# Final sums opened earlier and gMLP run ahead of the first keys in a cached attention block beside a gMLP mixer

## The chip, the cores and the metric

The kernel runs on 1 core of one Trainium2 chip. The metric is device time in microseconds (us): the median of several executions. A profile of one further execution gives a trace of every engine. The engines are named PE (TensorE, matrix products), PEld (its weight loads), DVE (VectorE), ACT (ScalarE), POOL (GpSimd) and SP (SyncE, which here only issues transfers). Sixteen DMA engines move the data between HBM and the on-chip memory.

## The reference

The output is the sum of the input, a decode step of attention over a cache, and a gMLP mixer, for 4 batch rows of width 640. Keys and values have 32 heads, 4096 positions and 128 columns each, in bf16: 134 MB of keys and as much of values.

```python
def _A_ref(x, k_cache, v_cache, wq, wo):
    B, Sq, D = x.shape
    Hq, Dh = (32, 128)
    ...
    q = (lambda x, *d: x.transpose(*d))((x @ wq).reshape(B, Sq, Hq, Dh), 0, 2, 1, 3)
    ...
    scores = jnp.einsum('bhqd,bhkd->bhqk', q, k) * Dh ** (-0.5)
    p = _softmax(scores, axis=-1)
    o = jnp.einsum('bhqk,bhkd->bhqd', p, v)
    return (lambda x, *d: x.transpose(*d))(o, 0, 2, 1, 3).reshape(B, Sq, Hq * Dh) @ wo

def _B_ref(x, w_in, w_sp, b_sp, w_out):
    ...
    z = _gelu(jnp.einsum('bsd,df->bsf', x, w_in))
    z1 = z[..., :Fh].copy()
    z2 = _layernorm(z[..., Fh:], axis=-1)
    g = jnp.einsum('ts,bsf->btf', w_sp, z2) + b_sp[None, :, None]
    return jnp.einsum('bsf,fd->bsd', z1 * g, w_out)
x = A_x
xn = _layernorm(x, axis=-1)
return x + _A_ref(xn, A_k_cache, A_v_cache, A_wq, A_wo) + _B_ref(xn, B_w_in, B_w_sp, B_b_sp, B_w_out)
```

The query is one position long (Sq = 1), so nearly all the bytes are read once and used once. wq is 640 x 4096, wo 4096 x 640, w_in 640 x 1728, w_out 864 x 640.

## The kernel before

**Tiles.** Heads are taken in 4 groups of 8; a tile is one batch row of one group, so there are 16 tiles (`NT`). The keys of a tile are one run of 8,192 KB (64 KB in each of 128 partitions), its values another. A tile of keys is worked on in 4 quarters.

**The ring.** One large buffer, `ring`, has 11 units of 16 KB per partition (L91). A run of keys takes 4 units, a run of values 4. `place_k` (L102) puts the keys of tile 0, 2, 4... at units 3 to 6 (`K_EVEN`) and those of tile 1, 3, 5... at units 0 to 3; the two share unit 3, and `quarters` (L105) gives the order in which a tile's quarters are worked on, so that the shared unit comes free first. Values lie at units 7 to 10 (`V_HOME`). At the start wq holds units 0 to 2, and gMLP's weights units 9 and 10 (`W_UNIT`); at the end the last values take units 3 to 6 and wo units 0 to 2.

**The queue.** All large transfers go out on SP's queue in the order in which they are written down in `loads` (L189 to L201): k0, gMLP's weights, k1, v0 in two halves, k2, then v1, k3, v2, k4 and so on, the last values in two halves, wo in four pieces. wq goes out ahead of them all (L110). `pump` (L206) issues the next entries of the list as far as the units that they need have been given up in the program's order; the issue itself then waits on SP until the engines have really finished with these units. SP works in order: what stands behind a waiting issue waits too. k0 goes out in two halves (`load_k`, L148), gMLP's weights in four transfers (`load_w`, L132: w_in 2,160 KB, w_out 960 KB, and two edge pieces of 60 KB).

**One quarter of keys.** `product` (L537, DVE) multiplies the quarter in place with the query, `fold` (L546, DVE) adds the upper half of the 128 columns to the lower, `sums` (L552, PE) adds 64 columns down to 8 with 8 products by the identity into one of two `s_ps` buffers, and `row_sums` (L567, DVE) adds the 8. After the fourth quarter `lane_max` (L577: DVE's `m`, a small ACT step, a PE product into `max_ps`) and `exps` (L585: DVE's `nb`, then the exponential on ACT) make the probabilities `p`; `deal` (L602, ACT) spreads them over the heads' columns, or `deal_part` (L615, DVE) in the last tile.

**Values.** `blocks` (L626, PE) multiplies the dealt probabilities of tile i - 1 with its values, in two halves, behind the second and third quarter of tile i; `gather` (L642) brings the result together. Per group of four tiles `group_den`, `group_rden`, `group_norm`, `group_turn` and `group_pick` divide by the sum of the exponentials and turn the result; `group_den` (L690) has a POOL step `own_sum` and a PE product `den`.

**gMLP.** `gmlp_in` (ACT copies of edge columns, 90 PE products with w_in), `gmlp_gelu`, `gmlp_stats` and `gmlp_out` (18 PE products with w_out, added to `out_ps`) are written into tile 0: behind its third quarter's sums, behind its fourth's, and between `lane_max(0)` and `exps(0)`.

**The end.** `open_finals` (L668) takes both `s_ps` buffers for the final sums, clears them on DVE (L673), copies the sums so far (the input and gMLP) from `out_ps` to `rest` (L676, DVE) and puts them into the final sums with PE products (L680). It comes after the last tile's deals. Then follow `group_den`, `group_rden`, the last `blocks`, `gather`, the group's steps, and `pair_proj` (L748), 128 PE products with wo's two halves. Two copies and two stores end the program.

The engines work in the order in which the program is written (`manual_schedule`, L760), each in its own.

Of the kernel before, what the change touches and what calls it, by code (L numbers as in the profile page):

```python
# [9 lines left out]
FP32 = mybir.dt.float32  # L10
# [10 lines left out]
def kernel(  # L21
# [14 lines left out]
    nc = tc.nc  # L36
    P = nc.NUM_PARTITIONS
    Bsz, Sq, D = A_x.shape
# [10 lines left out]
    HG = H // HT  # L49
    NT = HG * Bsz  # L50
# [3 lines left out]
    NQ = 4  # L54
# [3 lines left out]
    UNIT = QC * Dh  # L58
    UV = UC // QC
# [12 lines left out]
    NOH = D // 2  # L72
# [9 lines left out]
    work = ctx.enter_context(tc.tile_pool(name="work", bufs=1))  # L82
# [16 lines left out]
    K_EVEN, V_HOME = NQ - 1, 2 * NQ - 1  # L99
    W_UNIT, WO_UNIT = V_HOME + UV, 0  # L100

    def place_k(i):  # L102
        return 0 if i % 2 else K_EVEN

    def quarters(i):  # L105
        return tuple(reversed(range(NQ))) if place_k(i) == 0 else tuple(range(NQ))

    wq_flat = ring[:, 0 : DC * HD]
    wq_sb = wq_flat.rearrange("p (c n) -> p c n", n=HD)
# [38 lines left out]
    def load_k(i):  # L148
        t = units(place_k(i), NQ)
        step = (UV if i == 0 else NQ) * UNIT  # L150
        for e in range(0, NQ * UNIT, step):
            nc.sync.dma_start(out=t[:, e : e + step], in_=run_view(A_k_cache, i)[:, e : e + step])
        k_tiles[i] = t.rearrange("p (c d) -> p c d", d=Dh)

# [24 lines left out]
    def plan(keys, first, fn, *args):  # L179
        loads.append((keys, first, fn, args))  # L180

    def plan_k(i):
        plan([("k", i, q) for q in range(NQ)], place_k(i), load_k, i)

    def plan_v(i, part, unit, n=1):
        keys = [("v", i, part + e // UV) for e in range(n * UV)]
        plan(keys, unit, load_v, i, part, unit, n)

    plan_k(0)  # L189
    plan(["w"] * UV, W_UNIT, load_w)  # L190
    plan_k(1)
    plan_v(0, 0, V_HOME)
    plan_v(0, 1, V_HOME + UV)
    plan_k(2)
    for i in range(1, NT - 1):
        plan_v(i, 0, V_HOME, 2)
        if i + 2 < NT:
            plan_k(i + 2)
# [5 lines left out]
    used = set()  # L204

    def pump():  # L206
        while loads:
            keys, first, fn, args = loads[0]
            spots = range(first, first + len(keys))
            for u, key in zip(spots, keys):  # L210
                if u in holder and holder[u] != key and holder[u] not in used:
                    return
            holder.update(zip(spots, keys))
            fn(*args)
            loads.pop(0)
# [140 lines left out]
    def out_sum(half):  # L356
        return out_ps[OG * half : OG * half + Bsz, :]
# [26 lines left out]
    def gmlp_in():  # L384
        zT = gm["zT"] = ps_pv.tile([P, 2, NFC, Bsz], FP32, tag="pv", name="zT")
        w_cols = w_sb[:, 0 : DC * F].rearrange("p (a f) -> p a f", a=DC * 2)
        nc.gpsimd.memset(w_edge[:], 0.0)
        for g in range(2):
            at = NFF * P + g * TL * TR
            cols = w_cols[:, :, at : at + TL * TR].rearrange("p a (k e r) -> p a r e k", e=NW, r=TR)  # L390
            for r in range(TR):
                nc.scalar.copy(
                    out=w_edge[:, :, r, g * CW : g * CW + TL].rearrange(
                        "p a (e k) -> p a e k", e=NW
                    ),
                    in_=cols[:, :, r],
                )
        for t in range(2):
            w_t = w_cols[:, :, 0 : NFF * P].rearrange("p a (f k) -> p a k f", k=NFF)
            for k in range(NFC):  # L400
                for c in range(DC):
                    nc.tensor.matmul(  # L402
                        out=zT[: P if k < NFF else TN, t, k, :],
                        lhsT=w_t[:, 2 * c + t, k, :] if k < NFF else w_edge[:, 2 * c + t, k - NFF, :],
                        rhs=xnT[:, c, 0:Bsz],
                        start=(c == 0),
                        stop=(c == DC - 1),
                    )
# [104 lines left out]
    def stage_q(hg):  # L513
        ps = slice(hg % 2 * 2 * QW, (hg % 2 + 1) * 2 * QW)
        qr_ps = ps_m.tile([HT * Bsz, Dh], FP32, tag="m", name="qr_ps")
        for hh in range(QH):
            nc.tensor.matmul(  # L517
                out=qr_ps[:],
                lhsT=place[ps, hh, :],
                rhs=q_sb[ps, hg // 2, hh * Dh : (hh + 1) * Dh],  # L520
                start=(hh == 0),
                stop=(hh == QH - 1),
            )
        q_rows = small.tile([HT * Bsz, Dh], BF16, name="q_rows")
        nc.scalar.copy(out=q_rows[:], in_=qr_ps[:])  # L525
        qb_ps = ps_m.tile([P, Bsz, Dh], FP32, tag="m", name="qbc_ps")
        for b in range(Bsz):
            nc.tensor.matmul(
                out=qb_ps[:, b, :], lhsT=q_lanes[:, b, :], rhs=q_rows[:], start=True, stop=True
            )  # L530
        qbcs[hg] = small.tile([P, Bsz, Dh], BF16, name="qbc")
        nc.scalar.copy(out=qbcs[hg][:], in_=qb_ps[:])
# [130 lines left out]
    def out_last(part):  # L663
        half, c = divmod(part, 2)
        at = OG * (2 * c + half)
        return finals[c][at : at + Bsz, 0:NOQ]

    def open_finals():  # L668
        rest = work.tile([P, NOH], FP32, tag="early", name="rest")
        for c in range(2):  # L670
            f = ps_s.tile([P, QC, RW], FP32, name="s_ps")
            finals.append(f[:].rearrange("p c d -> p (c d)"))
            nc.vector.memset(finals[c][column_half(c), 0:NOQ], 0.0)  # L673
        for half in range(2):
            ps = slice(OG * half, OG * half + Bsz)
            nc.vector.tensor_copy(out=rest[ps], in_=out_sum(half))  # L676
        for part in range(CG):
            half, c = divmod(part, 2)
            ps = slice(OG * half, OG * half + Bsz)
            nc.tensor.matmul(  # L680
                out=out_last(part),
                lhsT=ident_f[ps, ps],
                rhs=rest[ps, c * NOQ : (c + 1) * NOQ],
                start=True,
                stop=False,
            )
# [73 lines left out]
    with tc.manual_schedule(engines={E.PE, E.DVE, E.Activation, E.SP}):  # L760
        pump()
        stage_q(0)
        LAST = NT - 1
        for i in range(NT):
            order = quarters(i)
            ends = i // Bsz - 1 if i > Bsz and i % Bsz == 1 else None
            for n, q in enumerate(order):
                product(i, q)
                fold(i, q)
                if n:  # L770
                    row_sums(i, order[n - 1])
                if ends is not None and n == 1:
                    group_rden(ends)
                    group_norm(ends)
                elif ends is not None and n == 2:
                    group_pick(ends)
                sums(i, q)
                if i == 0 and n == 2:
                    gmlp_in()
                elif i == 0 and n == 3:  # L780
                    gmlp_gelu()
                if i % Bsz == Bsz - 1 and n == 1 and i // Bsz + 1 < HG:
                    stage_q(i // Bsz + 1)
                if ends is not None and n < 2:
                    (group_den, group_turn)[n](ends)
                if i and n in (1, 2):
                    blocks(i - 1, n - 1)
                    if n == 2:
                        gather(i - 1)
            row_sums(i, order[-1])  # L790
            lane_max(i)
            if i == 0:
                gmlp_stats()
                gmlp_out()
                used.add("w")
                pump()
            exps(i)
            if i == LAST:
                deal_part(i, 0)
                deal_part(i, 1)  # L800
            else:
                deal(i)
        assert not loads
        open_finals()
        group_den(HG - 1)
        group_rden(HG - 1)
        blocks(LAST, 0)
        blocks(LAST, 1)
        gather(LAST)
        group_norm(HG - 1)  # L810
        group_turn(HG - 1)
        group_pick(HG - 1)
        for j in range(NP):
            pair_proj(j)

        res = work.tile([P, NOH], BF16, name="res")
        nc.scalar.copy(out=res[:OUT, 0:NOQ], in_=finals[0][column_half(0), 0:NOQ])
        nc.vector.tensor_copy(out=res[:OUT, NOQ:NOH], in_=finals[1][column_half(1), 0:NOQ])
        out_v = out.flatten_outer_dims()
        nc.scalar.dma_start(out=out_v[:, NOH:D], in_=res[OG : OG + Bsz])  # L820
        nc.sync.dma_start(out=out_v[:, 0:NOH], in_=res[0:Bsz])
# [30 lines left out]
```

## Time and profile before

| what | value |
|---|---|
| median of 3 runs | 661.39 us (661.39 to 661.72) |
| the profiled execution | 662.4 us |
| its span, first to last instruction | 660.3 us |
| busy: DVE | 496.9 us (75%) |
| busy: PE | 317.4 us (48%) |
| busy: ACT | 86.1 us (13%) |
| busy: POOL | 8.5 us (1%) |
| mean granted PE clock | 0.672 |
| bytes read from HBM | 282.24 MB, 427 GB/s over the span |

Times in the views of the profile count from the span's start. A busy share is an average over the whole span; it does not say which engine a stretch waits for. In a timeline line, "x8" means that so many instructions were merged, the arrow shows what is written from what, and the bracket at the end gives the idle time of that engine before the line and what ended it. SP's lines are the issues of transfers; the data lands later.

### The profile page before, as it was taken

Reading aid. Unit: us, or ns where it says so; the run is one execution under the profiler, and the core shown is the slowest. Engines: PE = TensorE matmul, PEld = TensorE weight load, DVE = VectorE, ACT = ScalarE, POOL = GpSimd, SP = SyncE. Lnnn points to the kernel's source line nnn. Section 1 sums busy time; section 2 is a strip of 40 time slices with the busy share of each in tenths; the row PEclk is TensorE's granted clock in tenths of the full one; section 3 lists DMA queues with packets and bytes.
Section 4 is the critical chain, followed back from the end, with each engine's and each line's share of the span. In section 5 each row is a group of like instructions: output and inputs, shape, how many; then the busy total and the mean of one; then the engine's idle time right before and its main releaser. Section 6 shows DMA issues by size and latency. Waiting matters only on the chain.

```text
span 660.3 us, 4884 instructions
## 1 busy us (share of the span) xinstructions
PE 317.4 (48%) x2095; PEld 146.0 (22%) x2095; DVE 496.9 (75%) x287; ACT 86.1 (13%) x208; POOL 8.5 (1%) x31
## 2 busy tenths in 40 slices
PE   0357552806346273634627064462716447272557
PEld 0114120302213131221303032130312213021225
DVE  2497968959496895949679595977949498794961
ACT  0023120020202002020200202011020200202000
POOL 3000000000000000000000000000000000000000
PEclk9765595756868575686857668585577857557777
DMA  9999999999999999999999999999999999999996
GB/s 379 431 451 414 441 434 445 418 445 433 430 437 442 417 438 433 437 442 445 405 438 433 445 438 441 409 442 433 430 445 445 418 437 434 421 445 438 409 429 276
DMA packets 6137, 282.56 MB, mean 428 GB/s; under 512 B 696, under 2 KB 836, under 8 KB 1124
## 3 DMA queue, kind: packets, MB, share of 16 engines
q1 hardware_dynamic: 6096, 282.24, 98.9%
q8 instruction: 16, 0.26, 0.1%
q10 hardware_dynamic: 20, 0.01, 0.0%
q14 instruction: 5, 0.04, 0.0%
HBM read 282.24 MB, written 0.01 MB: 427 GB/s over the span
## 4 chain that ended last, share of the span: by engine, by line
DMA 64%; DVE 23%; PE 12%; issue 1%; ACT 0%; SPq 0%; DVEq 0%; ACTq 0%
DMA ring<-in_A_k_cache_dram 64%; DVE ring L539 14%; PE s_ps L557 9%; DVE ring L548 7%; PE pv_acc L632 1%; PE zT L402 1%; PE s_ps L751 1%; DVE s_sb L570 0%; DVE pm L617 0%; PE s_ps L680 0%; PE pv L649 0%; PE max_ps L583 0%; DVE m L579 0%; PE o_ps L720 0%; PE den L699 0%
## 5 line engine op out<-in xcount | busy, mean ns | idle before, releaser
L539 DVE TENSOR_TENSOR ring<-ring,qbc 128x8192 bf16<-128x8192 bf16 x64 | 282.7, 4418 | 81.2 <-DMA ring<-in_A_k_cache_dram 81.2
L557 PE MATMUL s_ps<-ring,ident 128*128 128x512 bf16 x512 | 186.8, 531 | 250.1 <-DVE ring L548 250.1
L548 DVE TENSOR_TENSOR ring<-ring 128x4096 bf16<-128x4096 bf16 x64 | 146.7, 2292 | 2.2
L557 PEld LDWEIGHTS <-ident 128*128 128x128 bf16 x512 | 63.6, 128 | 356.5 <-issue 255.8
L632 PE MATMUL pv_acc<-ring,pm 128*32 128x512 bf16 x1024 | 84.0, 484 | 28.7 <-DMA ring<-in_A_v_cache_dram 28.7
L570 DVE TENSOR_REDUCE s_sb<-s_ps 128x64 f32<-128x512 f32 x64 | 43.9, 686 | 32.4 <-PE s_ps L557 32.4
L632 PEld LDWEIGHTS <-pm 128*32 128x32 bf16 x1024 | 44.5, 148 | 64.4 <-issue 56.8
L645 ACT COPY pv_sb<-pv_acc 128x512 f32<-128x512 f32 x16 | 9.4, 586 | 366.5 <-PE pv_acc L632 366.5
L604 ACT ACTIVATE pm<-p,hmask 128x256 bf16<-128x256 bf16 x120 | 49.5, 494 | 0.5
L649 PE MATMUL pv<-sel,pv_sb 128*128 128x8 f32 x128 | 16.9, 259 | 11.1 <-ACT pv_sb L645 11.1
L649 PEld LDWEIGHTS pv<-sel,pv_sb 128*128 128x128 f32 x128 | 15.5, 191 | 18.3 <-ACT pv_sb L645 18.3
L583 PE MATMUL max_ps<-lay,head_scale 128*128 128x16 f32 x32 | 6.7, 287 | 25.3 <-ACT lay L581 25.3
L581 ACT ACTIVATE lay<-lane_diag,m 128x16 f32<-128x16 f32 x16 | 4.9, 307 | 77.2 <-DVE m L579 77.2
L583 PEld LDWEIGHTS max_ps<-lay,head_scale 128*128 128x128 f32 x32 | 5.2, 203 | 34.3 <-ACT lay L581 34.3
L589 DVE TENSOR_REDUCE nb<-max_ps 128x1 f32<-128x16 f32 x16 | 2.8, 174 | 12.6 <-PE max_ps L583 12.6
L692 POOL TENSOR_TENSOR own_sum<-acc,hmask 128x32 f32<-128x32 f32 x4 | 2.0, 500 | 623.0 <-ACT p L593 623.0
L593 ACT ACTIVATE p<-s_sb,nb 128x256 bf16<-128x256 f32 x16 | 8.1, 508 | 10.8 <-DVE nb L589 10.7
L525 ACT CAST q_rows<-qr_ps 32x128 bf16<-32x128 f32 x4 | 1.0, 255 | 58.4 <-PE qr_ps L517 58.4
L579 DVE TENSOR_REDUCE m<-s_sb 128x1 f32<-128x256 f32 x16 | 6.7, 420 | 0.5
L709 DVE TENSOR_TENSOR o_n<-pv,rden 128x32 bf16<-128x32 f32 x4 | 0.8, 191 | 7.7 <-PE pv L649 7.6
L343 PE MATMUL q_ps<-ring,xnT 128*32 128x512 bf16 x40 | 4.5, 631 | 4.1 <-DMA ring<-in_A_wq_dram 4.1
L327 PE MATMUL xnT_ps<-ident,xn_bf 4*128 4x4 bf16 x5 | 0.4, 178 | 11.6 <-DVE xn_bf L315 11.6
(95 smaller groups left out, 88.1 us busy)
## 6 DMA issues: line engine op xcount, KB each, us to landing
ring<-in_A_v_cache_dram SPq DMA_DIRECT2D x4, 4096.0 KB, 16.0
ring<-in_A_k_cache_dram SPq DMA_DIRECT2D x2, 4096.0 KB, 29.4
ring<-in_A_wq_dram SPq DMA_DIRECT2D x1, 5120.0 KB
ring<-in_A_wo_dram SPq DMA_DIRECT2D x1, 2560.0 KB
ring<-in_B_w_in_dram SPq DMA_DIRECT2D x1, 2160.0 KB, 38.1
ring<-in_A_wo_dram SPq DMA_DIRECT2D x1, 1920.0 KB, 17.6
ring<-in_B_w_out_dram SPq DMA_DIRECT2D x1, 960.0 KB
ring<-in_A_wo_dram SPq DMA_DIRECT2D x1, 480.0 KB, 18.2
```

The lines of the kernel that those rows point to most:

```text
L402: nc.tensor.matmul(out=zT[: P if k < NFF else TN, t, k, :], lhsT=w_t[:, 2 * c + t, k, :] if k < NFF else w_edge[:, 2 * c + t, k - NFF, :], ...
L539: nc.vector.tensor_tensor(out=t, in0=t, in1=qbcs[i // Bsz][:, i % Bsz, None, :].to_broadcast([P, QC, Dh]), op=ALU.mult,)
L548: nc.vector.tensor_tensor(out=t[:, :, 0:HD2], in0=t[:, :, 0:HD2], in1=t[:, :, HD2:Dh], op=ALU.add)
L557: nc.tensor.matmul(out=s[:], lhsT=ident[:], rhs=t[:, :, g * RW : (g + 1) * RW], start=(g == 0), stop=(g == n - 1),)
L570: nc.vector.tensor_reduce(out=scores[i][:, q * QC : (q + 1) * QC], in_=sums_ps.pop((i, q))[:], axis=AX.X, op=ALU.add,)
L579: nc.vector.tensor_reduce(out=m1[:], in_=scores[i][:], axis=AX.X, op=ALU.max)
L583: nc.tensor.matmul(out=ps[:], lhsT=head_scale[:], rhs=d[:], start=True, stop=True)
L593: nc.scalar.activation(out=p[:], in_=scores.pop(i)[:], func=ACT.Exp, bias=nb[:], scale=scale_qk, accum_out=acc[hg % NACC][:, b : b + 1],)
L604: nc.scalar.activation(out=p_m[i % 2][:, :, h, :], in_=probs[i][:].rearrange("p (n c) -> p n c", c=BC), func=ACT.Copy, scale=hmask[:, h : ...
L632: nc.tensor.matmul(out=pv_acc[g * CW : (g + 1) * CW, :], lhsT=pm[:, b0 // BC, :, :].rearrange("p h (k c) -> p c (h k)", k=GC)[:, c, :], rh ...
L645: nc.scalar.copy(out=pv_sb[:], in_=pv_acc[:])
L649: nc.tensor.matmul(out=pvs[hg][:, :, b], lhsT=pv_sb[:, k * Dh : (k + 1) * Dh], rhs=sel[:, k, :], start=(k == 0), stop=(k == GC - 1),)
```

## The change

Three places are edited.

1. Order and place of the first transfers. gMLP's weights go out ahead of k0. k0 lies at units 4 to 7 in place of 3 to 6, and its quarters are worked on from the last to the first; its upper half is loaded first. v0 goes out as one run, like the later ones, in place of two halves. In all the program has 48 transfers in place of 49.
2. gMLP's four steps run ahead of tile 0 in place of in it, on every engine that they use.
3. The copy of the sums so far to `rest` becomes a function of its own, `keep_rest`, and runs in tile 0 behind the second quarter; `rest` gets memory of its own. The other steps of `open_finals` run in the last tile between `lane_max` and `exps`; `group_den` of the last group runs ahead of the deals in the program's order.

```diff
     def place_k(i):
-        return 0 if i % 2 else K_EVEN
+        return NQ if i == 0 else 0 if i % 2 else K_EVEN
 
     def quarters(i):
-        return tuple(reversed(range(NQ))) if place_k(i) == 0 else tuple(range(NQ))
+        return tuple(range(NQ)) if place_k(i) == K_EVEN else tuple(reversed(range(NQ)))
...
         step = (UV if i == 0 else NQ) * UNIT
-        for e in range(0, NQ * UNIT, step):
+        for e in reversed(range(0, NQ * UNIT, step)):
...
+    plan(["w"] * UV, W_UNIT, load_w)
     plan_k(0)
-    plan(["w"] * UV, W_UNIT, load_w)
     plan_k(1)
-    plan_v(0, 0, V_HOME)
-    plan_v(0, 1, V_HOME + UV)
-    plan_k(2)
-    for i in range(1, NT - 1):
+    for i in range(NT - 1):
         plan_v(i, 0, V_HOME, 2)
         if i + 2 < NT:
             plan_k(i + 2)
...
+    rest = work.tile([P, NOH], FP32, name="rest")
+
+    def keep_rest():
+        for half in range(2):
+            ps = slice(OG * half, OG * half + Bsz)
+            nc.vector.tensor_copy(out=rest[ps], in_=out_sum(half))
+
     def open_finals():
-        rest = work.tile([P, NOH], FP32, tag="early", name="rest")
         for c in range(2):
...
-        for half in range(2):
-            ps = slice(OG * half, OG * half + Bsz)
-            nc.vector.tensor_copy(out=rest[ps], in_=out_sum(half))
         for part in range(CG):
...
         stage_q(0)
+        gmlp_in()
+        gmlp_gelu()
+        gmlp_stats()
+        gmlp_out()
+        used.add("w")
+        pump()
         LAST = NT - 1
...
-                if i == 0 and n == 2:
-                    gmlp_in()
-                elif i == 0 and n == 3:
-                    gmlp_gelu()
...
+                if i == 0 and n == 1:
+                    keep_rest()
...
             lane_max(i)
-            if i == 0:
-                gmlp_stats()
-                gmlp_out()
-                used.add("w")
-                pump()
+            if i == LAST:
+                open_finals()
             exps(i)
             if i == LAST:
+                group_den(HG - 1)
                 deal_part(i, 0)
                 deal_part(i, 1)
...
-        open_finals()
-        group_den(HG - 1)
         group_rden(HG - 1)
```

## The prediction

> **What bounds the kernel now.** I read the totals first, then the chain of waits, then the timeline of both ends, and last the transfers with their landing times.
>
> ```profile
> span 660.3 us, 4884 instructions
> q1 hardware_dynamic: 6096, 282.24, 98.9%
> ```
>
> The sixteen DMA engines are taken up for 98.9% of the span. VectorE (DVE), the busiest engine, is at 75%. So this is a stream of transfers with work beside it; the chain of waits shows its beat:
>
> ```profile
> 112.38 28.17 DMA ring<-in_A_k_cache_dram
> ...
> 140.57 4.43 DVE ring L539
> ...
> 145.03 2.30 DVE ring L548
> ...
> 147.37 3.58 PE s_ps L557 x8
> 150.98 28.17 DMA ring<-in_A_k_cache_dram
> ```
>
> The columns are start, length, and who held the chain. The chain reads 28.17 us of DMA and 10.4 us of compute, which looks like a loop with compute in it. It is none: during those 10.4 us the previous values still stream. One beat is 150.98 - 112.38 = 38.60 us for one key run and one value run, 16,384 KB: 424.5 KB per us, and I use that rate below. An edit inside the beat is worth nothing; one counts only if it makes the stream run dry, or if it lies behind the stream's end.
>
> The front, from the timeline:
>
> ```profile
> 16.39 4.46 PE L343 MATMUL q_ps<-ring,xnT 128*32 128x512 bf16 x40 [4.05 <-DMA ring<-in_A_wq_dram]
> 26.09 4.43 DVE L539 TENSOR_TENSOR ring<-ring,qbc 128x8192 bf16<-128x8192 bf16 x1 [4.92 <-DMA ring<-in_A_k_cache_dram]
> 40.93 2.38 ACT L392 COPY ring<-ring 128x160 bf16<-128x160 bf16 x6 [17.79 <-DMA ring<-in_B_w_in_dram]
> 50.18 4.42 PE L402 MATMUL zT<-xnT,ring 128*128 128x4 bf16 x90
> 63.82 4.42 DVE L539 TENSOR_TENSOR ring<-ring,qbc 128x8192 bf16<-128x8192 bf16 x1
> 74.22 0.33 SPq L152 DMA_DIRECT2D ring<-in_A_k_cache_dram  x1
> ```
>
> wq has landed at 16.39, k0's first half at 26.09, w_in at 40.93; k1's first product starts at 63.82, and k2 is issued at 74.22. The tail:
>
> ```profile
> 636.58 1.75 SPq L175 DMA_DIRECT2D ring<-in_A_wo_dram  x4
> 642.29 0.99 DVE L676 COPY rest<-out_ps 4x320 f32<-4x320 f32 x2
> 642.81 1.21 PE L680 MATMUL s_ps<-rest,ident_f 4*4 4x160 f32 x8 [4.29 <-DVE rest L676]
> 644.52 6.25 PE L632 MATMUL pv_acc<-ring,pm 128*32 128x512 bf16 x64
> 653.55 3.86 PE L751 MATMUL s_ps<-ring,o_r 128*4 128x160 bf16 x128
> ```
>
> TensorE (PE) ends at 657.41; 2.9 us of copying and storing the result follow. Two more views say what else is there:
>
> ```profile
> ring<-in_A_wo_dram SPq DMA_DIRECT2D x1, 1920.0 KB, 17.6
> ring<-in_A_wo_dram SPq DMA_DIRECT2D x1, 480.0 KB, 18.2
> ```
>
> ```profile
> 655.50:656.00 0.50, 0.50 (x24) 0.50 (x19) 0.00 (x0) 0.00 (x0) 0.00 (x0) 0.50 0.08 28
> ```
>
> The columns of the first view are the transfer's size and its time from issue to landing; of the window, busy time of PE, its weight loads, DVE, ACT and POOL, then PE's granted clock, the DMA share, GB/s. The last four wo transfers are issued at 636.58, 636.97, 637.44 and 637.90 (the timeline cut fine), so the second lands at 636.97 + 17.6 = 654.6, the third at 655.6, and the fourth (160 KB, 18.1 us in the same view) at 656.0. At 655.5 the stream is nearly empty and PE works without a break at clock 0.50. So the tail is bound by PE's chain now, and 1.4 us behind it lies a second bound: wo's landing.
>
> **Part 1, the tail (L665-686, L797-809).** Before, PE's four opening products (L680, 1.21 us) and the denominator (0.64 us at 643.95) wait for the two `rest` copies, which stand on DVE behind the deals (L617, 639.41 to 641.81). After, `rest` is copied during tile 0, and the opening products follow the maximum's product, done at 638.53: 638.53 + 1.21 = 639.74. DVE's two memsets (0.49 us) slip in between 637.74, the end of `m`, and 638.56, the start of `nb`: cover 0.8 us, so nothing. POOL's own_sum ends at 639.45 + 1.28 = 640.73; the denominator behind it at 641.4. The first deal is done at 639.41 + 1.20 = 640.6. So the last values' products start at 641.4 in place of 644.52, 3.1 us earlier. Their second half starts at 641.4 + 3.1 = 644.5; its values land 5,120 / 424.5 = 12.1 us ahead of wo's last, at 643.9, with 0.6 us to spare. The products end at 641.4 + 6.37 = 647.8, and 2.78 us of gathering, normalising and turning (650.77 to 653.55, unchanged) put the final projection at 650.5. Its first half of wo lands 2,560 / 424.5 = 6.0 us ahead of 656.0, at 650.0: in time. Its 64 products take 1.93 us (half of 3.86). Then PE stands until 654.6, for wo's second transfer. The 64 products left, at the row's pitch ((3.86 - 0.23) / 127 = 28.6 ns, 0.23 for the last alone), end at 654.6 + 63 x 0.0286 + 0.23 = 656.6 in place of 657.4: **-0.8 us** of the 3.1. Bounds: the very last four products wait for 656.0, so no better than 656.3, -1.1; if landing counts for more than I read, 0.
>
> On the clock: the window above has PE at 0.50 though it had not paused for over 0.8 us since 642.81. The Trainium skill ("TensorE: Matmul & The Clock Gate", the section on the HAM clock gate) has the half rate come after an idle window of about 3.4 us and end after about 3.4 us of sustained work; by that rule these products would run at full rate and end at 656.3, and the sum below would be -1.2 in place of -0.9. The row disagrees with the rule here, so I take the row.
>
> **Part 2, one transfer fewer (L148-152, L189-194).** v0 goes as one run of 8,192 KB. What a transfer costs in a full stream: k0's first half (9,216 KB behind the start, 21.7 us at the beat's rate) landed 4.3 us behind that line; v0's second part (issued 66.67, 16.0 to landing: 82.7; 32,936 KB, 77.6 us) 5.1 us behind it. At most 0.8 us went astray over about seven transfers: 0.1 each, **-0.1 us**. Bounds: 0, and -0.6 if all but a little of the loss came of the split.
>
> **Part 3, the front: gMLP ahead of the keys.** SP's queue is now wq, w_in, w_out, two edge pieces, k0's two halves, k1, v0. k0's second half is queued behind a wait for wq's landing (the order of the changed kernel shows eight completion semaphores used in turn), at 16.4; queued work lasts to 5,120 + 3,240 + 4,096 KB = 29 us, so nothing. k1 no longer shares a unit with k0 and goes out after PE's use of wq (20.9), not at 36.49; that gains nothing either, as the stream was full then. Behind k1 stands v0, which waits for gMLP's last product and k0's first quarter (some 45 us); behind v0 stands k2. k1 streams until 60: covered.
>
> The cost is that DVE starts later. w_in lands at 7,280 / 424.5 + 4.3 = 21.5; k0's first half at 12,456 / 424.5 + 4.3 = 33.6 (26.0 before). gMLP until then: ACT is free at 23.15, its six copies (2.38) end at 25.5, the 50 of 90 weight products behind the last copy at 49 ns (4.42 / 90) end at 28.0. The gelu (54.70 to 57.10: 2.4 us) makes 30.4, and sums and gate (60.24 to 63.82: 3.6 us) 34.0. DVE's first product starts at 34.0, not 26.1. Tile 0 then takes 27.9 us to its last fold (566.56 to 594.49 in tile 14), 0.8 for the `rest` copies (L676, overlapped), 0.04 + 3.57 for the last sums, 2.1 to the end of `nb` (597.92 to 600.06): 34.4. k1 starts at 68.4, only 4.6 us later than before, as gMLP's steps no longer stand in the tile; k2 goes out 10.4 us behind that (63.82 to 74.22), at 78.8.
>
> Is that in time? v0 lands at 82.6 as before. A transfer sent into an empty queue lands its length plus a fixed time after issue: 2.2 us for x (issued 0.73, first used 2.95), 3.6 for wq, the very first large one (16.39 - 0.73 - 12.06). So k2 must go out by 80.4, or by 79.0. I take x's row, since wq's carries the start of the program: **0 us**, with 1.6 us to spare; bounds 0 and +0.5 (3.6 us, and v0 landing 0.7 earlier). Without that cover each us of lateness costs one us, as the stream never makes anything up. What is late next: v1 goes out at 88.35 + 4.6 = 93.0 and is wanted 3.6 us ahead of k2's landing (101.95), at 98.3. k1's tile ends at 68.4 + 33.5 = 101.9, even with k2's landing; from there on the beat is the old one.
>
> **Sum:** -0.8 - 0.1 + 0 = -0.9 us. The profiled execution took 662.4 us with a span of 660.3; its span should become 659.4. The runs' median is 661.39, 1.0 below the profiled time; less 0.9 it is **660.5 us**.
>
> **Rivals.**
> *The stream gains too.* The loss of 0.8 us between the two landings in part 2 goes for the most part (-0.6), and the tail reaches its bound (-1.1): 659.7. For it: the loss falls in the stretch that is rearranged. Against: five of its transfers stay.
> *k2 comes too late (slower).* Place: SP's issue of k2; price: one us per us behind 80.4. It decides if k2 goes out over 2.2 us behind its deadline (1.3 beyond the 0.9 gained). Two table loads of 1.28 us (Tanh and Sqrt) lay in the shadow of other work at 43.33 and 59.67; in the open they make k2 go out at 81.4, with the 3.6 us price 2.4 us late: 661.39 - 0.9 + 2.4 = 662.9. Against: ACT is free ahead of each, and started both early before.
> *The tail gains nothing,* because PE's end is set by wo's landing already: 661.3. Against: in the windows PE has no pause from 653.55 on while the stream dries up.
> *Each transfer has a fixed price of its own,* 2.2 us by x's row: 661.39 - 0.8 - 2.2 = 658.4. Against: a beat of 38.60 us with two transfers cannot hold it. The Trainium skill ("DMA: Bandwidth & Descriptors", Anatomy of one DMA) fits 2.0 us plus bytes / 436e3 to one transfer, on another issuing path; in this queue it would be overlapped.
>
> **Chances.** Forecast 0.52, no tail gain 0.08; both are within 0.2% (1.3 us, about what a measurement of this kernel can tell from no change): same 0.60. Stream gains 0.22, fixed price 0.02: faster 0.24. k2 late 0.16: slower. The forecast's own range is 660.1 to 661.3. The eight-in-ten range runs from 659.6, with the first rival in it, to 662.2, which takes in the late k2 with up to 1.7 us of loss.
>
> **What would show it.** Tail: PE's last-value products start near 641.4 on the old scale, L751 comes in two pieces with about 2 us between, released by wo's transfer. Front: first product near 34, k1's near 68.4, k2's issue near 79, and k2's landing still near 102. If k2's first product starts after 102.6, the second rival is at work. If PE ends before wo's last landing plus 0.3 us, or L751 shows no pause, part 1 is wrong.

## The result, and the profile after

| what | before | after |
|---|---|---|
| median | 661.45 us (661.38 to 662.34, 6 runs) | 664.15 us (663.61 to 664.42, 6 runs) |
| the profiled execution | 662.4 us, span 660.3 | 664.25 us, span 662.2 |
| last keys' first product to PE's end | 605.24 to 657.41: 52.17 us | 607.67 to 659.47: 51.80 us |

The ratio is 1.0037 [1.0026, 1.0048]: the changed kernel is 2.7 us slower. 660.5 us was predicted, with 659.6 to 662.2 as the range.

The totals after, from the page (the last lines are queue, packets, MB, share of the sixteen engines):

```profile
span 662.2 us, 4881 instructions
...
q1 hardware_dynamic: 5952, 282.24, 98.8%
q8 instruction: 16, 0.26, 0.1%
```

The share of the stream is the same to a tenth of a per cent, over a longer span. So for the most part the same bytes took longer *while the engines count as taken up*; a plain gap of 1.9 us would have lowered the share by 0.3 points. The front of the changed kernel, from its timelines:

```profile
15.93 4.46 PE L340 MATMUL q_ps<-ring,xnT 128*32 128x512 bf16 x40 [3.67 <-DMA ring<-in_A_wq_dram]
...
33.81 4.42 DVE L536 TENSOR_TENSOR ring<-ring,qbc 128x8192 bf16<-128x8192 bf16 x1
...
68.30 4.42 DVE L536 TENSOR_TENSOR ring<-ring,qbc 128x8192 bf16<-128x8192 bf16 x1
...
78.69 0.33 SPq L152 DMA_DIRECT2D ring<-in_A_k_cache_dram  x1
...
103.19 4.42 DVE L536 TENSOR_TENSOR ring<-ring,qbc 128x8192 bf16<-128x8192 bf16 x1 [1.33 <-DMA ring<-in_A_k_cache_dram]
```

First product 33.81 (34.0 predicted), k1's 68.30 (68.4), k2's issue 78.69 (78.8): every time that was worked out for the engines came true. Only the last line did not. k2's first product waits for its transfer and starts at 103.19; 101.95 was the landing of before. The prediction's own sign for the late k2, a start after 102.6, is there, though k2 went out 1.7 us ahead of the deadline that it had set.

The delay grows along the stream: the last keys' first product is 2.4 us later than before (607.67 against 605.24). From there on the tail is 0.4 us shorter than that of the execution of before that was profiled. That execution was itself an unlucky one, as the experiments show; against a second trace of the kernel before (e8, 51.04 us) the tail is 0.8 us longer.

### The profile page after: what moved, and what is told of

Its sections match the earlier page's. It is cut to its first block, busy times and chain, and to the rows that moved or that the text cites. A ratio compares the mean times of both kernels' runs of the same rounds, so it can differ in the third digit from the quotient of the medians.

```text
span 662.2 us, 4881 instructions
## 1 busy us (share of the span) xinstructions
PE 316.2 (48%) x2095; PEld 144.8 (22%) x2095; DVE 497.0 (75%) x287; ACT 86.0 (13%) x208; POOL 8.4 (1%) x31
## 4 chain that ended last, share of the span: by engine, by line
DMA 71%; PE 19%; DVE 8%; ACT 1%; issue 1%; SPq 0%; DVEq 0%
DMA ring<-in_A_v_cache_dram 66%; PE pv_acc L629 11%; PE s_ps L554 6%; DVE ring L536 5%; DMA ring<-in_A_wo_dram 3%; DVE ring L545 2%; DMA ring<-in_A_wq_dram 2%; PE q_ps L340 1%; PE zT L399 0%; DVE s_sb L567 0%; PE s_ps L751 0%; ACT ring L389 0%; PE pv L646 0%; DVE rest L670 0%; DVE q_sb L347 0%
## 5 line engine op out<-in xcount | busy, mean ns | idle before, releaser
L554 PE MATMUL s_ps<-ring,ident 128*128 128x512 bf16 x512 | 184.9, 526 | 249.2 <-DVE ring L545 249.2
```

The costliest lines, as they stand in the source:

```text
L554: nc.tensor.matmul(out=s[:], lhsT=ident[:], rhs=t[:, :, g * RW : (g + 1) * RW], start=(g == 0), stop=(g == n - 1),)
```

## The experiments

Each ran beside the kernel before on the same chip; the medians of before were 661.41 to 661.46 us in the three groups. Edits are against the changed kernel unless said otherwise.

**The tail alone (e1), on the kernel before.** The new tail goes onto the old front, and `rest` is copied in tile 2, clear of the front.

```diff
...
+                if i == 2 and n == 1:
+                    keep_rest()
...
+            if i == LAST:
+                open_finals()
             exps(i)
             if i == LAST:
+                group_den(HG - 1)
...
-        open_finals()
-        group_den(HG - 1)
```

> The kernel before with the tail edit alone (the sums so far are copied to rest in tile 2, the opening products and the denominator go ahead of the last deals); the front is the old one, k2 goes out at 74.2. Theory A (the front edit loses the time, because k2 goes out at 78.7, too close to the end of what is queued; the tail edit gains): faster than before by 0.4 to 0.8 us, 660.6 to 661.1, the stream as before (last keys used from 605.2). Rival B (the tail edit itself loses): slower than before, 662 or more.

661.91 us (661.53 to 662.08, 11 runs) against 661.44: 1.0006 [0.9997, 1.0015]. The gain that was expected is not there; if anything 0.5 us are lost, which the interval does not tell from nothing. Its PE at the end, from the timeline:

```profile
650.25 2.30 PE L754 MATMUL s_ps<-ring,o_r 128*4 128x160 bf16 x64
654.66 2.30 PE L754 MATMUL s_ps<-ring,o_r 128*4 128x160 bf16 x64 [2.10 <-DMA ring<-in_A_wo_dram]
```

The projection starts early, as predicted, and then stands 2.10 us for wo's second transfer. What that landing already meant to the old tail shows in e8, next.

**The kernel before once more (e8).** The unchanged kernel, one execution, for its trace.

> The kernel before once more, for its profile. Theory F (the first profiled execution, 662.4 against a median of 661.4, was 1 us long in its tail, as TensorE ran the last keys' sums at half clock, 3.3 us in place of 1.9, so that the tail had slack which the median has not): about 661.4, span near 659.3, and 51.1 to 51.3 us from the last keys' first product to TensorE's end, in place of 52.2. Rival G (the us lies elsewhere): 52.2 us again.

661.35 us, span 659.2. From its timeline, and below it the line of the first trace of before that answers to its first line:

```profile
633.31 1.89 PE L557 MATMUL s_ps<-ring,ident 128*128 128x512 bf16 x8
...
652.10 2.30 PE L751 MATMUL s_ps<-ring,o_r 128*4 128x160 bf16 x64
654.57 1.80 PE L751 MATMUL s_ps<-ring,o_r 128*4 128x160 bf16 x64 [0.16 <-DMA ring<-in_A_wo_dram]
```

```profile
633.22 3.33 PE L557 MATMUL s_ps<-ring,ident 128*128 128x512 bf16 x8 [1.24 <-DVE ring L548]
```

In the first trace these eight products took 3.33 us, here 1.89. The whole tail (last keys' first product at 605.32 to PE's end at 656.37) is 51.04 us, not 52.17. So an execution of the kernel before that takes the median's time already waits for wo, by 0.16 us, in the middle of its projection. There was nothing to gain. The new tail only moves PE's wait: the second half starts at 654.66 in e1 and at 654.57 here. It then takes 2.30 us against 1.80; these 0.5 us are as much as e1 lost, though one trace of each cannot show that they are always so.

**The front alone (e2).** The changed kernel with the old `open_finals` and its place at the end; no `keep_rest` in tile 0.

```diff
...
-                if i == 0 and n == 1:
-                    keep_rest()
...
-            if i == LAST:
-                open_finals()
...
+        open_finals()
+        group_den(HG - 1)
```

> The changed kernel with the old tail (rest copied and the final sums opened behind the last deals); the front is the new one. Theory A: 664.15 plus the tail's 0.4, about 664.5, k2 issued near 78 (0.8 us earlier, as the copies to rest leave tile 0, so up to 0.8 us less loss: 663.7 to 664.5). Rival B (the tail loses): near 661.4.

661.34 us (661.05 to 663.32, 11 runs): 1.0000 [0.9991, 1.0008]. The new front by itself costs nothing; at least 663.7 had been expected of theory A, which took most of the loss for the front's own. From the timeline:

```profile
77.49 0.33 SPq L152 DMA_DIRECT2D ring<-in_A_k_cache_dram  x1
```

k2 goes out 1.2 us earlier than in the changed kernel, 0.9 of it for want of the `rest` copies in tile 0 (e5 moves these alone), and its first product starts at 101.99. Each part alone loses some 0.5 us at most; together they lose 2.7.

**k2 in two pieces (e3).** Three quarters of k2 do not need the unit that comes free last, and go out ahead.

```diff
+    def plan_k_parts(i):
+        for q0, q1 in ((1, NQ), (0, 1)):
+            keys = [("k", i, q) for q in range(q0, q1)]
+            plan(keys, place_k(i) + q0, load_k_part, i, q0, q1)
...
-        if i + 2 < NT:
+        if i == 0:
+            plan_k_parts(2)
+        elif i + 2 < NT:
```

> The changed kernel, with k2 sent in two pieces: the three units that only k0 held go out first (k0 is finished near 66), the one unit shared with k1 behind them at 78.7. All else is the changed kernel, gMLP first and v0 as one run; 49 transfers. Theory A (lateness of k2's issue): the loss goes, about 661.0 (661.45 less the tail's 0.4 to 0.8), k2's first product near 102 in place of 103.2, no slow stretch at 80 to 86. Rival C (the new order of transfers, or v0 as one run, makes the stream slower whatever the issue time): stays at 664.1.

661.61 us (661.32 to 661.97, 11 runs): 1.0 [0.9991, 1.0009]. SP's timeline:

```profile
66.75 12.63 SPq L158 DMA_DIRECT2D ring<-in_A_k_cache_dram  x2
```

The first piece goes out at 66.75, and 2.5 us of the loss are gone. All else of the change is in this kernel, so k2's issue is the place. The end of PE's work in it:

```profile
654.62 1.12 PE L764 MATMUL s_ps<-ring,o_r 128*4 128x160 bf16 x48 [3.25 <-DMA ring<-in_A_wo_dram]
655.92 0.70 PE L764 MATMUL s_ps<-ring,o_r 128*4 128x160 bf16 x16 [0.18 <-DMA ring<-in_A_wo_dram]
```

wo's landing sets the end here too, with the stream whole: the new tail has 3.25 us to spare and no use for them. So the 661.0 that was expected, with a gain of the tail in it, is missed by 0.6.

**v0 in halves (e4).** The 49th transfer put back.

```diff
-        plan_v(i, 0, V_HOME, 2)
+        if i == 0:
+            plan_v(0, 0, V_HOME)
+            plan_v(0, 1, V_HOME + UV)
+        else:
+            plan_v(i, 0, V_HOME, 2)
```

> The changed kernel with v0 in two halves as before, so 49 transfers; both halves go out near 44.3, k2 at 78.7 as in the changed kernel. Theory A: as the changed kernel, 664.1 within 0.3. Rival D (v0 as one run is what costs): 661 to 662. By the prediction's term of 0.1 us for a transfer: 664.25.

664.09 us (662.83 to 664.54, 5 runs): 1.0036 [1.0022, 1.005], the time of the changed kernel (664.15). One transfer more or fewer is not to be seen. (k2 goes out at 79.09 here, 0.4 us later than in the changed kernel; the table of issues below has e4 in its place.)

**The `rest` copies in tile 2 (e5).** The smallest edit: the two copies (L670) move out of the stretch ahead of k2's issue.

```diff
-                if i == 0 and n == 1:
+                if i == 2 and n == 1:
                     keep_rest()
```

> The changed kernel with one line moved: the two copies to rest (0.8 us on VectorE) run in tile 2 in place of tile 0. The new front, v0 as one run and the new tail stay. Theory A (k2's issue needs a lead of about two us on the first DMA engine that runs out, near 80; at 78.7 it had 1.3): k2 goes out near 77.8, the loss goes whole, 661.4 to 661.9, as the run with k2 in two pieces. Rival E (lateness costs us for us, as I had priced it): 0.9 us less than the changed kernel, 663.2. Rival C (the new order itself costs): 664.1.

662.27 us (661.7 to 663.4, 11 runs): 1.0016 [1.0007, 1.0025]. k2 goes out at 77.78, 0.9 us earlier, and 1.9 of the 2.7 us come back: two us per us. The 661.4 to 661.9 that was expected is missed by 0.4. The profiled execution (663.4, the slowest of the eleven) shows a delay of another kind, at the end:

```profile
645.74 3.31 PE L629 MATMUL pv_acc<-ring,pm 128*32 128x512 bf16 x32 [1.71 <-DMA ring<-in_A_v_cache_dram]
```

The second half of the last values came 1.71 us late. The transfers of the stretch 640 to 643 (queue, packets, MB, share):

```profile
q8 instruction: 1, 0.02, 1.9%
q14 instruction: 1, 0.01, 0.6%
```

Two packets of instructions went through the data engines there. In the packet records the larger one (16 KB, 0.93 us, from 641.40) stands on the engine that finished last; the packet behind it took 1.72 us in place of 1.21, and that engine's share of the values ended at 645.24, the next one's at 643.89. So part of e5's 0.4 us may not be k2's; this was read, not varied.

**How the loss depends on k2's issue (e6, e9, e10, e7), on the kernel before.** Its stream and its tail stay as they are. 4, 5, 6 or 8 copies into a tile that is not otherwise in use then (1.07 us each on DVE) stand ahead of tile 1's first product, and push k2's issue out in steps.

```diff
+                if i == 1 and n == 0:
+                    for _ in range(5):
+                        nc.vector.tensor_copy(out=spread[:], in_=ident[:]...)
```

> The kernel before, with four extra copies (1.07 us each, of a constant onto itself) on VectorE ahead of tile 1's first product, so that k2 goes out some 4.3 us later, near 78 to 78.5; nothing else is moved. Theory A: lead of 1.5 to 2 us, 661.4 to 663.4: at the edge. Rival C (it takes the new order): 661.4.

> The kernel before, with eight such copies: k2 goes out near 82.3 to 82.7, over 2 us behind the first engine's end of v0 (about 80). Theory A: a loss of about 2 us as in the changed kernel, and a further us for each us behind it, together 4.5 to 6.5: 666 to 668. Rival C: 661.4.

> The kernel before with five extra copies ahead of tile 1's first product: k2 goes out near 79.4, 0.6 us ahead of the first DMA engine's end of v0 (80.0), with the old order of transfers and the old tail. Step theory (a transfer that comes when engines are about to run dry pays a restart, about 2 us on the last engine, however little it is late): 663 to 664.2, as the changed kernel less its tail. Slope theory (the loss grows us for us from an issue at 78.2, the line through the run at 82.3 and its 4.1 us): 662.6.

> The kernel before with six extra copies: k2 goes out near 80.5, 0.5 us behind the first engine's end of v0. Step theory: about 664 (a restart of 2 us and 0.5 of idle engines). Slope theory: 663.7.

Measured: e6 661.84 (661.36 to 663.84, 10 runs), 1.0014 [1.0005, 1.0023]; e9 663.37 (662.25 to 663.77, 9), 1.0024 [1.0014, 1.0034]; e10 663.39 (662.81 to 663.9, 6), 1.0029 [1.0018, 1.0041]; e7 665.48 (665.35 to 665.73, 4), 1.0063 [1.0047, 1.0078]. In the packet records of all these kernels the first of the sixteen engines ends its share of v0 at 79.9 to 80.1 and the last at 82.1 to 82.4. Set against that, in order of k2's issue (the fourth column is the mean of the times at which the sixteen engines end their shares of k2, from the packet records of the one profiled execution; the medians are those of all runs):

| kernel | k2 issued | ahead of the first engine's end (80.0) | k2's end, mean of engines | k2's first product | median against before |
|---|---|---|---|---|---|
| e8, before | 74.02 | 6.0 | 100.1 | 102.17 | -0.1 |
| e2, front alone | 77.49 | 2.5 | 100.1 | 101.99 | -0.1 |
| e5, copies in tile 2 | 77.78 | 2.2 | 100.4 | 102.04 | +0.9, of it about 0.5 the tail's (e1) |
| e6, 4 copies | 78.35 | 1.6 | 100.8 | 102.29 | +0.4 |
| the change | 78.69 | 1.3 | 101.6 | 103.19 | +2.7, of it about 0.5 the tail's (e1) |
| e9, 5 copies | 79.05 | 0.9 | 101.5 | 103.33 | +1.9 |
| e4, v0 in halves | 79.09 | 0.9 | 100.8 | 102.26 | +2.7, of it about 0.5 the tail's (e1) |
| e10, 6 copies | 80.03 | 0.0 | 101.3 | 103.02 | +1.9 |
| e7, 8 copies | 82.31 | -2.3 | 103.6 | 105.63 | +4.1 |

0.7 us of lateness, from 78.35 to 79.05, takes the loss from 0.4 to 1.9; the next us costs nothing more; after that it is close to a us for each. e6 stands on the edge: seven of its ten runs took 661.36 to 662.67, three 663.13 to 663.84. It is a step, and it lies ahead of the moment at which the first engine runs dry. A price of a us per us, from a deadline set anywhere, would have given e9 some 1.0 us less than e10; their medians are equal, and the means of their runs (663.13 and 663.36) lie 0.2 us apart. e10's first product is no measure of k2: it follows DVE's own work without a wait, as six copies have made tile 1 that late. e7 lost less than the 666 that was the least expected. e4's profiled execution (663.38) was one of its two quickest.

What happens in the step shows in the windows from 80 to 88 us. The columns are length; busy time of PE, PEld, DVE, ACT and POOL; the granted PE clock; the DMA share; GB/s. The last two count a packet whole in the window in which it starts, so the share can exceed 1. In this order: e2, the changed kernel, e9 and e7.

```profile
80.00:88.00 8.00, 6.13 (x41) 2.31 (x41) 7.97 (x5) 0.00 (x0) 0.00 (x0) 0.68 1.05 453
```

```profile
80.00:88.00 8.00, 5.38 (x40) 2.06 (x40) 7.97 (x4) 0.00 (x0) 0.00 (x0) 0.79 1.04 387
```

```profile
80.00:88.00 8.00, 5.89 (x32) 2.05 (x35) 7.97 (x4) 0.00 (x0) 0.00 (x0) 0.50 1.06 406
```

```profile
80.00:88.00 8.00, 4.91 (x13) 1.64 (x12) 7.97 (x4) 0.00 (x0) 0.00 (x0) 0.50 0.75 283
```

With the packets cut at the window's edges, the sixteen engines are taken up for 1.00 of these 8 us in e2 and move 431 GB/s; in the changed kernel it is 0.95 and 352 GB/s, in e9 0.96 and 362, in e7 0.66 and 244. The kernel before has 1.00 and 431, as e2. So the changed kernel moves 79 x 8 = 0.63 MB less, or 1.5 us at the beat's rate of 424.5 KB per us (0.435 MB), and the mean end of k2 is 1.5 us late (101.6 against 100.1). The packets say how. About 0.4 of it is idle time: eleven engines go on to k2 at once, the other five, done with v0 by 80.6, get their first packet of k2 between 80.84 and 81.82. The other 1.1 us are slow packets: in the steady stream a packet of 64 KB takes 2.42 us on its engine, and the first two of k2 on each engine took 2.97 us on average in the changed kernel (up to 4.2), 2.91 in e9 and 2.43 in e2. k2's first product is 1.0 to 1.2 us late against the two executions of the kernel before (102.17 in e8, 101.95). Only in e7 did all sixteen engines stand idle. SP issues k2 there at

```profile
82.31 0.33 SPq L152 DMA_DIRECT2D ring<-in_A_k_cache_dram  x1
```

and the first packets on the sixteen engines start between 83.27 and 83.82, 0.96 to 1.51 us later. The Trainium skill ("DMA: Bandwidth & Descriptors", the section on latency and other measured facts) gives some 0.6 us to the first byte on this path; counted from the end of the issuing instruction (82.64) the trace agrees, with 0.63 us. In the changed kernel, where the engines were still busy with v0 at the issue, the five late ones got their first packet 2.2 to 3.1 us after it, so that an issue 1.3 us ahead of the first engine's end was too late for them. Why the first packets are slow as well, no run shows.

**The front with k2 in two pieces and the old tail (e11).** The best combination that these results suggest: e2's and e3's edits together.

```diff
...
+        if i == 0:
+            plan_k_parts(2)
...
+        open_finals()
+        group_den(HG - 1)
```

> The new front and v0 as one run, k2 in two pieces, and the old tail: the lead on the stream is at its largest and the tail's pause is gone. Theory A and F: no better than the kernel before, 661.2 to 661.5, since the stream is never dry in either and its end sets the end; if lead was still worth something in the front alone (661.34), it shows as 661.1 or less.

661.33 us (661.18 to 661.53, 11 runs) against 661.46: 0.9998 [0.9989, 1.0007]. With k2 safe the front loses nothing, and no version gained anything that can be told from the kernel before.

## Why the prediction was wrong

**What bounds the kernel: right.** It is a stream of transfers, and work inside the beat is free. e11 carries gMLP ahead of the keys, DVE starting 7.8 us later (33.87 against 26.09), at no cost.

**Part 1, the tail, -0.8 us: wrong, measured +0.5 (interval -0.2 to +1.0).** The step that failed is the comparison at its end: the products "end at ... 656.6 in place of 657.4". The new times were nearly right: the second half starts at 654.66 (e1) for a predicted 654.6, and ends at 656.96. (The sum also takes 6.37 us for the last values' products, where the row has 6.25.) The 657.4 was not: it came from an execution that lost 1.1 us in its tail (52.17 against 51.04 us in e8), 1.0 of which the prediction had noticed as the distance to the median without asking which stretch it lay in. The slack it priced was that execution's own delay. The third rival, that wo's landing sets PE's end already, was the true case. It had 0.08.

How little the clock can be counted on shows in the same stretch. The tail of the changed kernel, from PE's timeline:

```profile
643.50 6.56 PE L629 MATMUL pv_acc<-ring,pm 128*32 128x512 bf16 x64
650.82 1.06 PE L646 MATMUL pv<-sel,pv_sb 128*128 128x8 f32 x8 [0.75 <-ACT pv_sb L642]
652.16 0.65 PE L720 MATMUL o_ps<-o_n,spread 128*64 128x32 bf16 x16 [0.28 <-DVE o_n L709]
652.74 2.25 PE L751 MATMUL s_ps<-ring,o_r 128*4 128x160 bf16 x64
657.16 2.31 PE L751 MATMUL s_ps<-ring,o_r 128*4 128x160 bf16 x64 [2.18 <-DMA ring<-in_A_wo_dram]
```

The last 64 products took 2.31 us after a pause of 2.18; in e3, 48 of them took 1.12 us after a pause of 3.25 (23 ns each against 36). The prediction's 28.6 ns each lay between the two, and 0.5 us at the very end of the program hang on it. The rule that the prediction weighed (the Trainium skill, "TensorE: Matmul & The Clock Gate", the section on the HAM clock gate: a half rate after about 3.4 us of idling, a full one after as much sustained work) is not borne out here either. The granted clock was 0.50 from 644 to 648 us, within 6.56 us of unbroken products, 1.00 from 650 to 652, and 0.50 again from 654 on. The first 64 products of the projection ran at half pace (2.25 us), though PE had paused for no more than 0.75 us at a time before them.

**Part 2, one transfer fewer, -0.1 us: nothing measurable.** e4 puts it back at 664.09 against 664.15, with runs that spread over 1.7 us and k2 0.4 us later.

**Part 3, the front, 0 us: this is where the sign was lost.** Arrivals, gMLP's chain and the `rest` copies (0.8 us; 0.9 by e5's issue of k2) were all priced right, to k2's issue within 0.1 us. The step that failed is "k2 must go out by 80.4, or by 79.0", "with 1.6 us to spare; bounds 0 and +0.5". Three things in it were wrong, each shown by the runs above:
- *The deadline was set against v0's landing,* at 82.6. That is the end of the last of sixteen engines. The first one runs dry at 80.0, and the engines' mean end is 80.7.
- *The lead was taken as a round trip of 2.2 us ahead of the landing.* The runs put the start of the loss some 2 us ahead of the first engine's end, at an issue of about 78: 2.5 us cost nothing, 2.2 and 1.6 us about 0.4. The 78.8 that the prediction had worked out was already behind it.
- *The price was taken as a us per us.* It is a step: 1.9 us (e9) almost at once, without more for the next us (e10). An upper bound of +0.5 could not hold that.

The second rival, "k2 comes too late", was the right mechanism at the right place, with 0.16. Its condition was wrong, though: it asked for longer work ahead of k2's issue, and none was needed. The cover of 1.6 us that the forecast named was not there.

That the two parts meet is visible in no part alone. The front by itself (k2 at 77.49) stands just ahead of the step; the 0.9 us of copies, which belong to the tail, push it over.

**Why 1.0 to 1.2 us at k2 become 2.4 at the end: read from the packets, not varied.** A landing is that of the slowest engine. By the mean of the sixteen engines nothing more is lost behind k2: k2's shares end at 101.61 on average in the changed kernel against 100.10 in e8, those of the last keys at 605.08 against 603.57, 1.5 us later both times. What grows is the lag of the slowest engine behind that mean: from 1.2 us at k2's end to 2.2 at the last keys', where the two executions of the kernel before have 1.1 and 1.3. SP's issues of keys show two long beats, where 38.6 us is the usual:

```profile
113.59 0.33 SPq L152 DMA_DIRECT2D ring<-in_A_k_cache_dram  x1
153.07 0.33 SPq L152 DMA_DIRECT2D ring<-in_A_k_cache_dram  x1
...
462.04 0.33 SPq L152 DMA_DIRECT2D ring<-in_A_k_cache_dram  x1
502.30 0.33 SPq L152 DMA_DIRECT2D ring<-in_A_k_cache_dram  x1
```

They are 39.48 and 40.26 us, and the kernel before has one as well:

```profile
382.76 0.33 SPq L152 DMA_DIRECT2D ring<-in_A_k_cache_dram  x1
422.39 0.33 SPq L152 DMA_DIRECT2D ring<-in_A_k_cache_dram  x1
```

It is 39.63 us. A packet of instructions (16 KB, some 0.95 us of an engine, sixteen in a run) falls into each of these beats, but also into nearly all the others; it matters which engine it takes. In the beat of 40.26 us one starts at 475.48 on one of the two slowest engines, whose next share ends at 491.38, 20.7 us after the one before, where 19.3 is the usual; there the lag goes from 1.3 to 2.5 us. In the kernel before the packet at 475.4 left it at 1.4. At the last keys e9 and e4 end with lags of 2.5 and 2.4 us, e10 with 1.5. Whether the late k2 makes such a hit likelier, or it is luck, stays open.

## What to carry to other kernels

A transfer that must follow another without a gap has to be issued well before the *first* of the engines runs out of the one in front, not before that one's landing; here 2.5 us ahead cost nothing, 1 us cost about 2, and the loss came as a step. Before slack is priced from a profiled execution that lies above the median, find the stretch in which it lost the difference, with a second trace if there is one. Small work that is free in the steady beat, here 0.9 us of copies, is not free ahead of an issue that gates the stream.

## What the runs showed of the hardware that was not expected

- Engines can be nearly as taken up and move far less: 0.95 of the time at 352 GB/s against 1.00 at 431 in the same 8 us (packets cut at the window's edges), by first packets of 2.97 us in place of 2.43 above all, when the next transfer is issued 1.3 us rather than 2.5 us before the first engine runs dry.
- The sixteen engines end one 8,192 KB transfer spread over some 2.2 us (about 80.0 to 82.2), in every kernel here.
- A 16 KB packet of instructions on the engine that is last in a transfer delays the landing: in e5 that engine ended 1.35 us behind the next (645.24 against 643.89).
- The same eight products on the same data took 3.33 us in one execution of the kernel before and 1.89 in another.
